# Attention on row halves: ScalarE's copy of a finished product placed behind the transposes' copies, fewer DMAs begun per step, and the weight decoding moved to another place in the loop

## The chip, the cores and the metric

The kernel runs on one core of a Trainium2 chip. The metric is the device time of one execution in microseconds; lower is better. The core's engines are named as the profile names them: PE (TensorE, the matrix engine; PEld are its weight loads), DVE (VectorE), ACT (ScalarE), POOL (GpSimd) and SP (SyncE, which here begins DMAs and passes semaphores on). Each engine runs its own instructions in the order in which they were written and meets the others through semaphores.

## What is computed

Attention with queries averaged in twos, then a dense feed-forward layer, then a layer that sends every token to one of eight experts:

```python
q_pool = q.reshape(B, H, S // 2, 2, D).mean(axis=3)      # B 4, H 8, S 1152, D 64
scores = q_pool @ k.T / sqrt(D)
attn = exp(scores - max) / (sum + 1e-9)
x = (attn @ v), laid out as 2304 tokens x 512
h = x @ w_in; g = piecewise(h); x = g @ w_out            # 512 -> 2048 -> 512
expert = argmax(normalised x @ normalised emb.T / tau)
out = gate * (relu(x @ w1[expert]) @ w2[expert])
```

## The kernel before

**Three stages.** The attention runs from the start to about 476 us, the dense layer behind it, the experts last. The change touches the attention loop (`Attention.run`) and what is done beside it.

**Pairs and steps.** The loop goes through 16 pairs of heads (n from 0 to 15). The 576 pooled queries of both heads of a pair make 1152 rows, which are nine tiles of 128 rows; each tile is one step (t from 0 to 8, s = 9n + t). Tile t = 4 holds 64 rows of either head, the **mixed tile**, and its scores take 18 matmuls where the others take 9. All matmuls work on 64 contracted rows, so that the upper and the lower half of the PE array each carry their own stream; where both halves write one PSUM bank, a `nop` on SP passes the semaphore from one half to the other (`relay`, `order`, L251 to L258; L254 in the profile is that `nop`). PE therefore can't go on with the second half before SP has come to the `nop`, and SP runs it in its own order, between the DMAs that it begins.

**What one step does.** PE writes the scores of tile t into the tile `sc` (three PSUM banks, one buffer). DVE reads them (`peak`, L265), writes them to SBUF as `e` and keeps the extreme of each row. ACT takes the exponential (`exp`, L272). PE transposes the `e` of two steps ago into `pa` and `pb` (`turn`, L289). ACT copies these, rounded, to `pth` (L307, two instructions), and DVE subtracts to get the rest, `ptl` (L309, two instructions). PE also works on `av`, the products of the transposed tiles with v: groups of 288 columns, four to a pair (`av_group`, L322), 36 matmuls each, fed into the steps from a queue. When the last matmul of a group is written, ACT's copy of it to `avs` (L329) is written at once, and after every second group four DMAs of `avs` are queued (`store`).

**Written order inside a step.** Scores with `av` matmuls between them; `peak`; the transposes with `av` matmuls between them; the copies and subtractions of `parts`; then `send`; further `av` matmuls; `exp`; and last `aside(s)`, which holds work of the later stages.

**SP's DMAs.** `later` puts a DMA into a list with the step from which it may go, and `send(3)` begins up to three of them at the place named above. In a steady pair these are eight stores of `avs` (`av_b`, `av_t`), four of the rows' sums (`rs`), four loads of q and one of v (`vr`).

**Decoding of weights.** `w_in` and `w_out` come as 64-bit numbers and are turned into 32-bit ones by DVE, 512 columns at a time in three instructions (`Weights.decode`: L556, L560, L564), followed by two instructions on POOL. For the first three of sixteen weight blocks (`EARLY`), that is 18 such DVE pieces, this happens beside the attention: in steps 74, 92 and 110 `ws.load` begins two 512 KB loads on SP directly, and in every step with s % 3 = 1 from step 76 on one piece is written, at the step's end.

**POOL** prepares q and k of the next pair (L180, L57, L182, L193) and splits v (L57, L214 of the tile `vh`) in the steps t = 2 and t = 7.

Of the kernel before, what the change touches and what calls it, by code (L numbers as in the profile page):

```python
# [46 lines left out]
EARLY = 3  # L47

GQ = 288
# [25 lines left out]
class Attention:  # L75
# [4 lines left out]
    def __init__(self, tc, q, k, v, xs, cn):  # L80
        self.tc, self.nc = tc, tc.nc
        self.q, self.k, self.v, self.xs, self.cn = q, k, v, xs, cn
        self.st = {}
        self.avq = [collections.deque() for _ in range(2)]
        self.queue = []

    def later(self, step, f):
        self.queue.append((step, f))
# [223 lines left out]
    def av_group(self, n, g):  # L312
        nc = self.nc
        h = g // 2
        c0 = g * GQ
        box = {}

        def mm(half, i):
            if half == i == 0:
                box["t"] = self.ps_v.tile([128, 512], F32, name="av", tag="av")  # L320
            p, r = (UP, LO)[half], self.pth if i < 9 else self.ptl
            m = nc.tensor.matmul(box["t"][:, 0:GQ], lhsT=self.vh[p, h * 9 + i % 9], rhs=r[p, i % 9, c0:c0 + GQ],  # L322
                                 start=half == i == 0, stop=half == 1 and i == 17)
            if half and i == 0:
                self.order(m, box["m"])
            if i == 17 and not half:
                box["m"] = self.relay(m)
            if i == 17 and half:
                nc.scalar.copy(self.avs[:, g * GQ:(g + 1) * GQ], box["t"][:, 0:GQ])  # L329
                if g % 2:  # L330
                    self.store(n, h)
            elif i == 17:
                self.avq[1].extend(lambda j=j: mm(1, j) for j in range(18))

        self.avq[0].extend(lambda j=j: mm(0, j) for j in range(18))

# [27 lines left out]
    def run(self, aside, tail, early):  # L364


        np_ = self.NPAIR
# [5 lines left out]
        g = collections.deque()  # L373
# [3 lines left out]
        for n in range(np_):  # L377
            for i in range(4):
                last = -(-GQ * (i + 1) // 128) - 1
# [5 lines left out]
        while s < nt + 1 or self.avq[0] or self.avq[1]:  # L385
            s += 1
            self.step = s
            n, t = divmod(s, 9)
            more = n + 1 < np_
            up = lo = ()  # L390
            if s < nt:
                if s > 3:
                    next(clear, None)
                if t in (2, 7):
                    self.split_v(n, t // 7)
                if more:
                    if t == 0:
                        sq.extend(self.split_qk(n + 1))
                    for _ in range(((2, 2, 0, 3, 1, 2, 1, 0, 3) if n else (0, 0, 0, 0, 3, 3, 2, 2, 4))[t]):
                        if sq:  # L400
                            sq.popleft()()
                    if t == 7:
                        self.later(s + 1, lambda n=n: self.load_v(n + 1))
                    for h, m in (((0, 1),) if s == 2 else ((1, 1),) if s == 3 else ()) + (
                            ((t // 7, n + 2),) if n + 2 < np_ and t in (3, 7) else ()):
                        if s == 3 and m == 1:
                            self.load_k(1, 1)
                        for p in (UP, LO):
                            self.later(s + (m > 1 and n == 0) * 4, lambda a=(m, h, p): self.load_q(*a))
                if s < 3:  # L410
                    self.warm(WARM[s])
                up, lo = self.scores(n, t)
            for a in ready.get(s, []):
                self.av_group(*a)
            count = 18 if s > nt + 1 else 6 if t in (2, 3, 4) else 9
            left = [count + held - 1, count]

            def av(half, m=1):
                for _ in range(min(m, left[half], len(self.avq[half]))):
                    left[half] -= 1  # L420
                    self.avq[half].popleft()()

            for f in lo[:1]:
                f()
            av(0, held)
            for i, f in enumerate(up):
                if i + 1 < len(lo):
                    lo[i + 1]()
                else:
                    av(1)  # L430
                f()
            if s < nt:
                self.peak(n, t)
            if 2 <= s < nt + 2:
                (a, b), ps = self.turn(*divmod(s - 2, 9))
                if s >= nt:
                    av(1, 4)
                for i in range(6):
                    b[i]()
                    a[i]()  # L440
                av(1)
                for i in (6, 7, 8):
                    a[i]()
                for _ in range(4):
                    av(1)
                    av(0)
                for i in (6, 7, 8):
                    b[i]()
                self.parts(*divmod(s - 2, 9), ps)
            go = s >= nt - 7 and len(g) > 0 and g[0][0]()  # L450
            self.send(3)
            while any(min(left[half], len(self.avq[half])) for half in range(2)):
                av(1)
                av(0)
            held = int(bool(self.avq[0]))
            if s < nt:
                self.exp(n, t)
            for f in first[s + 1] if s < 3 else ():
                f()
            if 9 <= s < nt + 9 and t == 0:  # L460
                self.divisor(n - 1)
            if 9 <= s < nt + 9 and t == 1:
                self.sums(n - 1)
            if s == nt - 1:
                self.ps_s.release()
                early()
            if s == nt - 9:
                self.prep.release()
                g.extend(tail())
            if go:  # L470
                for f in g.popleft()[1]:
                    f()
            aside(s)
# [1049 lines left out]
def tile_kernel(tc, q, k, v, w_in, w_out, emb, tau, w1, w2, out):  # L1523
    nc = tc.nc
    with ExitStack() as ctx:
# [19 lines left out]
        with ExitStack() as actx:  # L1545
# [8 lines left out]
            for h in range(2):  # L1554
                at.load_first(h)
            rt = Router(tc, one, dram, emb, tau, cn)
            last = (at.NPAIR - 1) * 9
            pieces = []

            def aside(s):  # L1560
                if s == 12:
                    late["consts"] = rt.consts(stage)
                if 12 <= s < 12 + 3 * 6 and s % 3 == 0:
                    next(late["consts"], None)
                if s == 28:
                    late["emb"] = rt.experts(stage)
                if s in (31, 34):
                    late["emb"][(s - 31) // 3]()
                j, c = divmod(s - (last - 63), 18)
                if 0 <= j < EARLY:  # L1570
                    if c == 2:
                        ws.load(j)
                    elif c == 3:
                        pieces.extend(ws.decode(j))
                if pieces and s % 3 == 1:
                    pieces.pop(0)()

            def tail():
                late["x0"] = tc.alloc_tile_pool(name="x0", bufs=1, side="right", reuse_waits="tile")
# [96 lines left out]
```

## Time and profile before

| | us |
|---|---|
| median of three runs | 1151.37 |
| lowest and highest | 1150.55, 1151.93 |
| the profiled execution's own time | 1153.7 |
| its span, first to last instruction | 1151.9 |

The profile is of one execution. Its span is cut into views: groups of instructions by line, waits (who waited for whom), and a timeline of single instructions with their start, their duration and, in square brackets, the idle time of the engine just before, and what ended it. PE's granted clock is given as a share of its full 2.4 GHz.

| engine | busy in the span |
|---|---|
| PE | 95% |
| DVE | 74% |
| ACT | 66% |
| POOL | 38% |

### The profile page before, as it was taken

The page shows a single profiled execution, that of the slowest core. Times are in us where ns is not written, and L with a number is a line of the kernel's source. Part 1 is how long each engine was busy: PE and PEld are TensorE (multiplying, and loading weights), DVE is VectorE, ACT ScalarE, POOL GpSimd, SP SyncE. Part 2 cuts the span into 40 slices and gives each one's busy share as a digit, 9 for nine tenths or more (in the row PEclk, how much of TensorE's full clock was granted, in tenths as well). Part 3 has the DMA queues.
Part 4 walks back from the last instruction along what each step waited for, and adds up shares of the span by engine and source line. Part 5 has one row for each costly group of instructions (what it writes and reads, how often), then busy time and mean ns, then how long its engine had stood idle before and what let it go on. Part 6 is the DMA issues. An engine that isn't in the chain of part 4 may idle for free.

```text
span 1151.9 us, 27178 instructions
## 1 busy us (share of the span) xinstructions
PE 1098.8 (95%) x10276; PEld 999.3 (87%) x10276; DVE 856.8 (74%) x1620; ACT 758.0 (66%) x1432; POOL 441.1 (38%) x473
## 2 busy tenths in 40 slices
PE   8999899999898899999999999999999999999997
PEld 6888888888888888899999989998989899988887
DVE  5989889889899998689856764665355666777775
ACT  4888888878787888655554445544446466667664
POOL 5987667767676774500002131112010231122211
PEclk8999999999999999999999999999999999999999
DMA  6454444454545436555521212120222121187444
GB/s 157 116 137 117 112 111 113 115 143 111 148 112 148 112 77 174 153 179 172 165 83 46 77 53 74 42 69 20 86 90 92 47 84 49 49 277 244 143 153 133
DMA packets 76855, 132.01 MB, mean 115 GB/s; under 512 B 21031, under 2 KB 39079, under 8 KB 76704
## 3 DMA queue, kind: packets, MB, share of 16 engines
q1 hardware_dynamic: 67856, 103.48, 31.6%
q0 software_dynamic: 8544, 26.31, 8.0%
q8 instruction: 88, 1.44, 0.5%
q14 instruction: 63, 0.52, 0.2%
q10 hardware_dynamic: 304, 0.26, 0.1%
HBM read 140.08 MB, written 20.08 MB: 139 GB/s over the span
## 4 chain that ended last, share of the span: by engine, by line
PE 74%; DVE 11%; issue 5%; ACT 4%; SPq 2%; DMA 2%; POOL 1%; POOLq 0%; DVEq 0%; ACTq 0%
PE h L687 18%; PE y L719 17%; PE sc L238 9%; PE av L322 8%; PE d_po L1396 7%; PE d_ph L1362 6%; DVE e L265 5%; DVE ptl L309 3%; PE pa L289 3%; SPq L361 1%; PE d_ph L1376 1%; ACT pth L307 1%; ACT e L272 1%; PE pb L289 1%; DMA out<-d_ob,d_rec 1%
## 5 line engine op out<-in xcount | busy, mean ns | idle before, releaser
L238 PE MATMUL sc<-kT,qt 64*128 64x384 f32 x1440 | 200.2, 352 | 30.2 <-DVE e L265 23.1
L265 DVE TENSOR_SCALAR_CACHE_REDUCE e<-sc 128x1152 f32<-128x1152 f32 x144 | 194.9, 1353 | 40.1 <-PE sc L238 37.8
L238 PEld LDWEIGHTS sc<-kT,qt 64*128 64x128 f32 x1440 | 150.3, 188 | 52.6 <-DVE e L265 31.4
L272 ACT ACTIVATE e<-e,nm 128x1152 f32<-128x1152 f32 x144 | 182.4, 1266 | 15.6 <-DVE e L265 15.1
L322 PE MATMUL av<-pth,vh 64*128 64x288 f32 x1152 | 150.1, 313 | 2.8 <-SPq L254 2.6
L309 DVE TENSOR_TENSOR ptl<-pa,pth 128x768 fp32r<-128x768 f32 x144 | 137.3, 954 | 17.8 <-ACT pth L307 16.4
L1302 DVE TENSOR_TENSOR e<-e,e 128x512 fp32r<-128x512 f32 x200 | 129.6, 688 | 26.6 <-ACT e L1301 16.1
L322 PE MATMUL av<-ptl,vh 64*128 64x288 f32 x1152 | 145.3, 311 | 0.0
L706 DVE SCALAR_TENSOR_TENSOR u<-h,u 128x320 f32<-128x320 f32 (+1 forms) x112 | 55.9, 499 | 115.0 <-ACT u L705 115.0
L702 ACT ACTIVATE u<-h,half 128x320 f32<-128x320 f32 (+1 forms) x112 | 59.8, 534 | 118.1 <-PE h L687 118.1
L307 ACT CAST pth<-pa 128x768 fp32r<-128x768 f32 x144 | 115.3, 801 | 31.1 <-PE pa L289 28.6
L322 PEld LDWEIGHTS av<-pth,vh 64*128 64x128 f32 x1152 | 119.6, 187 | 6.8 <-SPq L254 6.7
L1396 PE MATMUL d_po<-e,e 128*128 128x512 f32 x504 | 120.6, 393 | 0.0
L322 PEld LDWEIGHTS av<-ptl,vh 64*128 64x128 f32 x1152 | 118.0, 187 | 0.0
L1301 ACT CAST e<-e 128x512 fp32r<-128x512 f32 x200 | 113.8, 620 | 0.3 <-issue 0.3
L719 PE MATMUL y<-wh,gh 128*128 128x512 f32 x288 | 113.9, 395 | 0.0
L719 PE MATMUL y<-wh,gl 128*128 128x512 f32 x288 | 113.7, 395 | 0.0
L719 PE MATMUL y<-wl,gh 128*128 128x512 f32 x288 | 113.6, 394 | 0.0
L1396 PEld LDWEIGHTS d_po<-e,e 128*128 128x128 f32 x504 | 92.8, 188 | 18.1
L289 PE MATMUL pb<-idf,e 64*128 64x64 f32 x864 | 101.2, 224 | 0.3
L652 POOL TENSOR_TENSOR xl<-xth,xl 128x512 f32<-128x512 f32 (+1 forms) x9 | 11.2, 1244 | 225.8 <-DMA xl<-av_b 127.6
L289 PE MATMUL pa<-idf,e 64*128 64x64 f32 x1728 | 88.7, 224 | 9.3 <-DVE ptl L309 9.2
(253 smaller groups left out, 2357.8 us busy)
## 6 DMA issues: line engine op xcount, KB each, us to landing
e<-moe_w SPq DMA_DIRECT2D x104, 512.0 KB
qr<-q SPq DMA_DIRECT2D x62, 288.0 KB
kr<-k POOLq DMA_DIRECT2D x60, 192.0 KB, 3.4
vr<-v SPq DMA_DIRECT2D x16, 576.0 KB
av_b<-avs SPq DMA_DIRECT2D x64, 128.0 KB
raw<-moe_w_in SPq DMA_DIRECT2D x14, 512.0 KB
raw<-moe_w_out SPq DMA_DIRECT2D x14, 512.0 KB
yt<-emb_rows SPq DMA_DIRECT2D x24, 256.0 KB
```

Source lines behind the costliest of these rows:

```text
L238: i = nc.tensor.matmul(s[:, j, 0:384], lhsT=qt[p, w, c:c + 128], rhs=d["kT", h][p, r], start=start, stop=stop)
L265: self.nc.vector.tensor_scalar(out=e.rearrange("p (a b) -> p a b", a=3), in0=d["sc"][:, :, 0:384], scalar1=-0.5 / D ** 0.5, scalar2=None, ...
L272: self.nc.scalar.activation(e, e, AF.Exp, bias=d["nm"][:, t:t + 1], scale=-1.0, accum_out=d["sum"][:, t:t + 1])
L289: x = nc.tensor.transpose(o, e[p, i * 128:(i + 1) * 128], idf[p, p])
L307: nc.scalar.copy(hi, p)
L309: nc.vector.tensor_sub(out=lo, in0=p, in1=hi.bitcast(F32))
L322: m = nc.tensor.matmul(box["t"][:, 0:GQ], lhsT=self.vh[p, h * 9 + i % 9], rhs=r[p, i % 9, c0:c0 + GQ], start=half == i == 0, stop=half == ...
L687: nc.tensor.matmul(ps[:, :n], lhsT=a[:, k], rhs=b[:, k, h0:h0 + n], start=i == 0, stop=i == 11)
L719: self.nc.tensor.matmul(y, lhsT=a, rhs=b, start=j == 0 and q == 0, stop=j == NF - 1 and q == 2)
L1301: self.nc.scalar.copy(hi, r)
L1302: self.nc.vector.tensor_sub(out=lo, in0=r, in1=hi.bitcast(F32))
L1396: self.nc.tensor.matmul(self.o, lhsT=(self.hh, self.hl)[a][f // 4][:, f % 4, s], rhs=self.w[b, f // 2][:, f % 2], start=f == 0 and q == 0, ...
```

## The change

Three edits, all in the attention.

**The copy.** Where the last matmul of a group is written, the copy to `avs` is no longer written at once but put into the list `full`, which the loop empties after `send` and the `av` matmuls behind it, ahead of `exp`. Three of a pair's four groups end behind `parts` already, so their copies stay where they were. The third group of the pair before ends early in step t = 4, ahead of `parts`; its copy moves behind the two copies to `pth`.

**The sends.** `send(3)` becomes `send(2)`, except in steps t = 3 and in the last pair, where it stays at three. The 17 DMAs of a pair have 19 places, where they had 27.

**The decoding.** The loads go through `later`, one part of 512 KB at a time, from step 37 on, each next one after the piece that frees its buffer. The pieces are written at the end of each step t = 3, that is ahead of the mixed tile's `peak`, from step 39 on, and from step 78 on also at the end of each step t = 6. Of the 18 pieces 11 stand at t = 3 and 7 at t = 6; the last is in step 132 (before: 127).

```diff
-                nc.scalar.copy(self.avs[:, g * GQ:(g + 1) * GQ], box["t"][:, 0:GQ])
-                if g % 2:
-                    self.store(n, h)
+                self.full.append(lambda: out(box["t"]))
...
+        def out(t):
+            nc.scalar.copy(self.avs[:, g * GQ:(g + 1) * GQ], t[:, 0:GQ])
+            if g % 2:
+                self.store(n, h)
...
-            self.send(3)
+            self.send(3 if t == 3 or n + 1 >= np_ else 2)
             while any(min(left[half], len(self.avq[half])) for half in range(2)):
                 av(1)
                 av(0)
             held = int(bool(self.avq[0]))
+            while self.full:
+                self.full.pop(0)()
...
+            def decode():
+                def load(part):
+                    at.later(at.step + 1, lambda: ws.load(*divmod(part, 2)))
+
+                def pieces():
+                    for j in range(EARLY):
+                        for i, f in enumerate(ws.decode(j)):
+                            f()
+                            part = 2 * j + i // 3 + 2
+                            if i % 3 == 2 and part < 2 * EARLY:
+                                load(part)
+                            yield
+                for part in range(2):
+                    load(part)
+                return pieces()
...
-                j, c = divmod(s - (last - 63), 18)
-                if 0 <= j < EARLY:
-                    if c == 2:
-                        ws.load(j)
-                    elif c == 3:
-                        pieces.extend(ws.decode(j))
-                if pieces and s % 3 == 1:
-                    pieces.pop(0)()
+                if s == 36:
+                    late["decode"] = decode()
+                if s > 36 and (s % 9 == 3 or s > 72 and s % 9 == 6):
+                    next(late["decode"], None)
```

ACT in steps t = 3 and t = 4 of pair 2, before; the first `exp` is that of the tile t = 3.

```order
L272 ACTIVATE e,sum<-e,nm 128x1152 [waits DVE_49,Activation_49]
L329 COPY avs<-av 128x288 [waits DMAHW4_49,DMAHW3_49,DMAHW5_49,DMAHW2_49,PE_49]
L307 CAST pth<-pa 128x2x6x64
L307 CAST pth<-pb 128x2x3x64 [waits PE_49]
L272 ACTIVATE e,sum<-e,nm 128x1152 [waits DVE_49,Activation_49]
```

The same place of the change:

```order
L272 ACTIVATE e,sum<-e,nm 128x1152 [waits DVE_49,Activation_49]
L307 CAST pth<-pa 128x2x6x64 [waits PE_49]
L307 CAST pth<-pb 128x2x3x64 [waits PE_49]
L334 COPY avs<-av 128x288 [waits DMAHW4_49,DMAHW5_49,DMAHW3_49,DMAHW2_49]
L272 ACTIVATE e,sum<-e,nm 128x1152 [waits DVE_49,Activation_49]
```

The copy and the two copies to `pth` have changed places; the `exp` of tile t = 4 now follows the copy.

DVE in pair 9 from the `peak` of tile t = 3 to that of t = 5, before; `wf` is a decoding piece.

```order
L265 TENSOR_SCALAR e,nm<-sc 128x1152
L309 TENSOR_TENSOR ptl<-pa,pth 128x2x6x64
L309 TENSOR_TENSOR ptl<-pb,pth 128x2x3x64
L265 TENSOR_SCALAR e,nm<-sc 128x1152
L309 TENSOR_TENSOR ptl<-pa,pth 128x2x6x64
L309 TENSOR_TENSOR ptl<-pb,pth 128x2x3x64
L556 TENSOR_SCALAR wf<-raw 128x512
L265 TENSOR_SCALAR e,nm<-sc 128x1152
```

The same place of the change:

```order
L265 TENSOR_SCALAR e,nm<-sc 128x1152
L309 TENSOR_TENSOR ptl<-pa,pth 128x2x6x64
L309 TENSOR_TENSOR ptl<-pb,pth 128x2x3x64
L561 TENSOR_SCALAR wf<-raw 128x512
L265 TENSOR_SCALAR e,nm<-sc 128x1152
L309 TENSOR_TENSOR ptl<-pa,pth 128x2x6x64
L309 TENSOR_TENSOR ptl<-pb,pth 128x2x3x64
L265 TENSOR_SCALAR e,nm<-sc 128x1152
```

The piece stands one tile earlier, between the subtractions of step t = 3 and the mixed tile's `peak`. PE's instructions keep their order in the whole program.

SP around the first pair of raw loads, before (steps t = 8 of pair 7 to t = 5 of pair 8; the `nop`s aren't shown):

```order
L165 DMA vr<-v 128x2x576
L153 DMA qr_4636<-q 64x1152 x2
L361 DMA av_b_73<-avs 64x512
L361 DMA av_t_76<-avs 64x64
L361 DMA av_b_73<-avs 64x512
L507 DMA raw<-moe_w_in 128x4x256
L512 DMA raw<-moe_w_out 128x1024
L361 DMA av_t_76<-avs 64x64
L351 DMA rs_b_79<-rt 9x32 x4
```

The same place of the change, and what is there now:

```order
L165 DMA vr<-v 128x2x576
L153 DMA qr_4718<-q 64x1152 x2
L364 DMA av_b_73<-avs 64x512
L364 DMA av_t_76<-avs 64x64
L364 DMA av_b_73<-avs 64x512
L364 DMA av_t_76<-avs 64x64
L354 DMA rs_b_79<-rt 9x32 x4
```

The two raw loads are gone from between the stores, which are begun in steps t = 2 and t = 3; `vr` is begun in step t = 0 of pair 8 (before: t = 8 of pair 7), with a q load behind it.

## Rows read from the trace of the kernel before

**Rows 1.** The page's head, and its busy times of the engines.

```profile
span 1151.9 us, 27178 instructions
PE 1098.8 (95%) x10276; PEld 999.3 (87%) x10276; DVE 856.8 (74%) x1620; ACT 758.0 (66%) x1432; POOL 441.1 (38%) x473
```

**Rows 2.** All peaks (duration min/median/max, first and last start); then busy times of stretches.

```profile
L265 DVE TENSOR_SCALAR_CACHE_REDUCE e<-sc x144: 1315/1358/1360, 10.0 to 465.2; 128x1152 f32<-128x1152 f32 x144
...
67.10:94.20 27.10, 25.69 (x402) 24.12 (x399) 24.59 (x38) 23.86 (x42) 22.27 (x36) 1.00 0.51 135
322.80:351.30 28.50, 25.68 (x404) 24.11 (x401) 26.54 (x41) 24.18 (x42) 21.07 (x23) 1.00 0.45 112
...
500.00:520.00 20.00, 20.00 (x113) 18.02 (x112) 17.28 (x35) 10.46 (x23) 0.00 (x0) 1.00 0.57 180
```

**Rows 3.** Timeline of DVE in pair 2: start, duration, instruction, idle time before.

```profile
67.09 1.36 DVE L265 TENSOR_SCALAR_CACHE_REDUCE e<-sc 128x1152 f32<-128x1152 f32 x1 [0.40 <-PE sc L238]
...
69.83 1.36 DVE L265 TENSOR_SCALAR_CACHE_REDUCE e<-sc 128x1152 f32<-128x1152 f32 x1
...
75.75 1.36 DVE L265 TENSOR_SCALAR_CACHE_REDUCE e<-sc 128x1152 f32<-128x1152 f32 x1 [0.28 <-PE sc L238]
...
79.21 1.36 DVE L265 TENSOR_SCALAR_CACHE_REDUCE e<-sc 128x1152 f32<-128x1152 f32 x1 [0.76 <-PE sc L238]
...
81.39 0.96 DVE L309 TENSOR_TENSOR ptl<-pa,pth 128x768 fp32r<-128x768 f32 x1 [0.81 <-ACT pth L307]
...
82.73 1.35 DVE L265 TENSOR_SCALAR_CACHE_REDUCE e<-sc 128x1152 f32<-128x1152 f32 x1
...
85.42 1.36 DVE L265 TENSOR_SCALAR_CACHE_REDUCE e<-sc 128x1152 f32<-128x1152 f32 x1
...
94.23 1.36 DVE L265 TENSOR_SCALAR_CACHE_REDUCE e<-sc 128x1152 f32<-128x1152 f32 x1 [0.37 <-PE sc L238]
```

**Rows 4.** Timeline of ACT in steps t = 4 and t = 5 of pair 2.

```profile
80.25 0.40 ACT L329 COPY avs<-av 128x288 f32<-128x288 f32 x1 [1.60 <-PE av L322]
80.55 0.81 ACT L307 CAST pth<-pa 128x768 fp32r<-128x768 f32 x1
81.25 0.49 ACT L307 CAST pth<-pb 128x384 fp32r<-128x384 f32 x1
81.61 1.28 ACT L272 ACTIVATE e<-e,nm 128x1152 f32<-128x1152 f32 x1
...
83.03 0.80 ACT L307 CAST pth<-pa 128x768 fp32r<-128x768 f32 x1
```

**Rows 5.** Waits in the attention: engine, line, waited for; total, times, longest.

```profile
POOL vh L57 <- PE av L322: 58.6, 15, 8.0
...
PEld sc L238 <- SPq L254: 14.0, 29, 1.5
...
POOL vh L57 <- DMA vr<-v: 9.0, 4, 2.6
```

**Rows 6.** Timeline of SP in pair 2: a third DMA of t = 2, and `vr`.

```profile
74.39 0.59 SPq L361 DMA_DIRECT2D av_b<-avs  x1
...
92.34 0.53 SPq L165 DMA_DIRECT2D vr<-v  x1
```

**Rows 7.** Timeline at the first raw loads (pair 8), and a stretch behind them.

```profile
242.70 0.48 SPq L512 DMA_DIRECT2D raw<-moe_w_out  x1
243.29 0.18 PEld L238 LDWEIGHTS sc<-kT,qt 64*128 64x128 f32 x1 [1.31 <-SPq L254]
...
245.00:249.00 4.00, 4.00 (x50) 4.00 (x49) 2.38 (x5) 2.00 (x4) 3.77 (x4) 0.71 0.91 293
```

**Rows 8.** The decoding pieces of DVE in the attention: duration min/median/max, first and last start.

```profile
L556 DVE TENSOR_SCALAR wf<-raw x6: 417/882/1529, 251.9 to 397.9; 128x512 uint32<-128x512 uint32 x6
L560 DVE SCALAR_TENSOR_TENSOR wf<-raw,wf x6: 1003/1009/1023, 260.4 to 407.5; 128x512 uint32<-128x512 uint32 x6
L564 DVE SCALAR_TENSOR_TENSOR wf<-raw,wf x6: 649/649/651, 270.1 to 417.3; 128x512 uint32<-128x512 uint32 x6
```

**Rows 9.** Timeline of POOL and of DVE at a piece in pair 10.

```profile
309.26 1.42 POOL L182 TENSOR_TENSOR qt<-qr,qt 128x576 fp32r<-128x576 f32 x1
```

```profile
309.87 1.09 DVE L556 TENSOR_SCALAR wf<-raw 128x512 uint32<-128x512 uint32 x1
```

More of the change, by code (lines that the diff above doesn't have):

```diff
@@ L84, in __init__ @@
         self.avq = [collections.deque() for _ in range(2)]
-        self.queue = []
+        self.queue, self.full = [], []
     def later(self, step, f):
@@ L1556, in tile_kernel @@
             rt = Router(tc, one, dram, emb, tau, cn)
-            last = (at.NPAIR - 1) * 9
-            pieces = []
+            def decode():
[12 more added lines that the diff above has]
+                return pieces()
             def aside(s):
```

## The prediction

> **What bounds the kernel now.** First the table of stretches [rows 2]: from 500 us on PE is busy 20.00 of 20 us, so from there on an earlier start is an earlier end by as much, and nothing in the change touches that part. The question is therefore how long the attention takes, and the last of its 144 peaks begins at 465.2 us [rows 2], of a span of 1151.9 [rows 1]. In the attention no engine is full: in pair 2, which no piece of decoding disturbs, PE is busy 25.69, DVE 24.59 and ACT 23.86 of 27.10 us [rows 2], and PE's busy time counts matmuls that overlap. What runs is a ring: DVE's peak frees `sc`, PE writes the next scores, DVE takes the next peak. The time between two starts of L265 is the step. Where DVE does nothing but its peak and two subtractions a step takes 69.83 - 67.09 = 2.74 or 85.42 - 82.73 = 2.69 us [rows 3]: DVE is the bound there. The rest is idle time of DVE, and the timeline names its end: 0.40 and 0.37 ahead of the peaks of t = 0, 0.28 ahead of t = 3, 0.76 ahead of t = 4, each for PE's scores, and 0.81 in t = 4 for ACT [rows 3]. The 0.76 is the mixed tile's double work on PE and stays. The other three are what the first two edits are about.
>
> **The copy.** In step t = 4 ACT stands idle 1.60 us ahead of the copy, until PE has done the last `av` matmul, and only then does the copy (0.40) and the two copies to `pth` (0.81 and 0.49) [rows 4]. `pa` is long there: in the next step the copy to `pth` begins 83.03 - 82.73 = 0.30 behind the peak [rows 3, 4], here 80.55 - 79.21 = 1.34. DVE waits 0.81 for it, and the step takes 82.73 - 79.21 = 3.52 instead of 2.7 [rows 3]. After the change `pth` comes at 0.30 behind the peak, about a microsecond earlier, and DVE's wait of 0.81 goes. What is late next? ACT's own turn: from 79.51 it does 0.81, 0.49, the copy 0.40 and an `exp` of 1.28, 2.98 together, and comes to the next `pa` at 82.49. The next peak would be at 79.21 + 2.71 = 81.92, and would want it at 82.22. ACT is 0.27 late, which at worst DVE waits for. So 0.54 to 0.81 a pair, and I take 0.70, since ACT's instructions overlap a little at their ends (81.61 is ahead of 81.25 + 0.49) [rows 4]. Fifteen pairs have such a copy (1 to 15): 15 x 0.70 = **10.5 us**, with 8.1 and 12.2 as the near ends. Should ACT stay late through the later copies of the pair, 0.3 is left of it, 4.5 us; ACT's 23.86 of 27.10 [rows 2] leave room, so I don't expect that. Who waits for the copy itself? It frees one of two `av` buffers, and the group that wants it begins two steps later; its DMAs come only after the next group.
>
> **The sends.** SP's `nop` stands behind the DMAs of the step. In t = 2 the third of them runs from 74.39 to 74.98 [rows 6], and behind it PE's second half is late; the peak of t = 3 finds DVE idle for 0.28, and that of t = 0, behind `vr` and loads of q, for 0.37 to 0.40 [rows 3]. All such waits of PE's weight loads for SP are 14.0 us in 29 places [rows 5]. With two DMAs the third's 0.6 us leaves the way of the `nop`, which is more than either wait. So 0.28 + 0.37 = 0.65 a pair for the pairs without decoding from 2 to 8: 7 x 0.65 = **4.5 us**. In pairs 9 to 13 DVE is late by its pieces and these waits are hidden; there I count nothing. The high end is all 14 pairs, 9 us; the low end 0, if a pair of DMAs still covers the `nop` in t = 0, where `vr` and a q load now go together, or in t = 3 with its three.
>
> **The raw loads.** In steps 74, 92 and 110 two loads go on SP behind the three of `send`, five in a row. At the first PE waits 1.31 us, and in the four microseconds behind it the granted clock is 0.71, so some of that stretch was at 1.2 GHz instead of 2.4 [rows 7]. Each of the three now goes within the two of a step. Saved: 1.31 less the usual 0.28 at the first, about half of that at the other two, and up to (1 - 0.71) x 4.0 = 1.2 of the clock: about **3.5 us**, from 1.5 (the waits of the first alone and little else) to 4.3 (three times 1.03 and all of the clock).
>
> **The decoding.** A pair with three pieces takes 28.50 against 27.10 [rows 2], 0.47 a piece of mean 0.85 [rows 8], because the pieces also fill DVE's waits. Eighteen pieces are 8.4, and about 1 more for first pieces that were longer than the least (L556: 0.42 to 1.53) [rows 8]: 9.4 us now. After the change 11 stand ahead of the mixed tile's peak, where DVE is idle for 0.76 in any case [rows 3]. Three are L564 with 0.65 and free, four L556 with a median of 0.88 (0.12 over), four L560 with 1.01 (0.25 over): 1.5 us. Seven stand at t = 6, ahead of a peak that has no idle time [rows 3], three L564, two L560, two L556: 5.7 us at full price, 3.4 at the share that a piece costs now. Together 5 to 7; saved **4 us**, from 2 to 4.5. POOL's two instructions behind every third piece stay as many.
>
> A piece can be held up, though. At 309.87 an L556 that takes 0.42 at best took 1.09; POOL's instruction beside it ran from 309.26 to 310.68 [rows 8, 9], and the piece ended 0.28 behind that. The Trainium skill (SBUF — State Buffer, section SBUF: two separate sides) states that a DVE instruction in a two-port mode, or with two SBUF inputs, and a GpSimd instruction lock one port pair against each other for their whole length, so that the later one waits; the trace agrees in this place. That would speak against the mixed tile, where POOL works without a pause; what it would give here is the second rival.
>
> **Sum.** 10.5 + 4.5 + 3.5 + 4 = 22.5 us. The profiled execution would go from 1153.7 to about 1131, the median, 2.3 lower, from 1151.4 to **1129**. All best ends give 30 (1121), all worst (4.5, 0, 1.5 and 0 for the decoding) 6 (1145).
>
> **Rivals.**
> *ACT takes DVE's place.* With the waits gone, ACT's four copies of a pair make its steps longer than 2.7, and the wait moves from t = 4 to t = 5 and on. Against it: 3.2 us of idle ACT in 27.1 [rows 2]. The copy then gives 4.5, the sum 16.5: 1135. Chance 0.17.
> *The pieces meet POOL.* If each of the 11 at the mixed tile takes as long as the longest L556, 1.53, then 0.77 of each is over, 8.5 instead of 1.5: the sum is 15.5, 1136. For it: POOL is busy 22.27 of 27.10 [rows 2], and rows 9. Against it: the least L556 of 0.42, and L564 always at 0.65 [rows 8]. Chance 0.13.
> *The sends do nothing.* The `nop` still comes too late, since a step's two DMAs take 1.1 us and the places are now 19 for 17. Then the first and last terms alone, and half of the raw loads': 1135 to 1140, say 1137. Chance 0.11.
> *`vr` comes too late, on the other side.* It was begun at 92.34 [rows 6], ahead of t = 0; it now goes a step later, 2.7 us. POOL waited for it already in 4 places, 9.0 us [rows 5]. Splitting v, and behind it q and k of the next pair, would begin up to 2.7 later in each pair. POOL has 27.1 - 22.3 = 4.8 us of room a pair [rows 2], and waits 58.6 us in 15 places for PE at the same instruction [rows 5]. The mechanism decides from the point where POOL's extra wait is more than those 4.8 in a pair; at 2 us over it in 14 pairs it costs 28 and the kernel takes 1157. Chance 0.04.
> *The change does next to nothing:* each idle time only moves to the next wait of the ring. Within 1149 to 1153. Chance 0.03.
> The forecast has the remaining 0.52.
>
> **How the numbers follow.** The range takes in the forecast with its best ends, with 2 us beyond for waits that shorten with the ring, and the first three rivals with room for two of them at once: 1119 to 1143. Beyond 0.2% (2.3 us, about what a measurement of this kernel can tell from no change) faster are the forecast and the first three rivals, 0.93; the same 0.03; slower 0.04.
>
> **What would show it.** In the profile after: the wait of L309 for ACT's L307 in t = 4 gone, and the step t = 4 to t = 5 at 2.7 to 2.9 instead of 3.5; if it is right but the next step has grown by 0.3 or more, the first rival. No idle time of DVE of 0.28 and 0.37 ahead of t = 3 and t = 0, and PE's waits for SP well under 14 us; if not, the third. No half clock after 240 us. L561 (the old L556) over 1.1 in several pieces of t = 3, with the mixed step over 3.5: the second. POOL's wait for `vr` far over 9 us, with the peaks of t = 0 or t = 4 waiting for q or k: the fourth. The forecast is wrong if the last peak begins later than 453, or if it begins near 443 and the end doesn't follow it, for then something behind the attention isn't bound by PE.

## The result and the profile after

| us | before | after |
|---|---|---|
| median (runs) | 1150.96 (4) | 1120.99 (4) |
| lowest and highest | 1149.44, 1151.93 | 1117.32, 1124.47 |
| span of the profiled execution | 1151.9 | 1119.8 |
| the last peak begins | 465.2 | 433.5 |
| behind that | 686.7 | 686.3 |

The changed kernel takes 0.974 of the time of the one before (95% interval 0.9707 to 0.9774), 30 us less, where 22.5 were forecast. The last two rows of the table show where: the attention is 31.7 us shorter, and what stands behind it is as long as it was.

The page's head and busy times, after, answer to [rows 1]:

```profile
span 1119.8 us, 27167 instructions
PE 1088.0 (97%) x10276; PEld 998.8 (89%) x10276; DVE 852.2 (76%) x1620; ACT 754.9 (67%) x1432; POOL 441.6 (39%) x473
```

The peaks (duration min/median/max, first and last start) and then busy times of stretches (length, PE, PEld, DVE, ACT, POOL, granted clock, DMA share, GB/s), after, answer to [rows 2]:

```profile
L265 DVE TENSOR_SCALAR_CACHE_REDUCE e<-sc x144: 1311/1357/1359, 9.8 to 433.5; 128x1152 f32<-128x1152 f32 x144
...
64.90:90.50 25.60, 24.79 (x400) 24.05 (x398) 24.50 (x39) 23.61 (x42) 22.40 (x37) 1.00 0.52 141
...
100.00:430.00 330.00, 315.44 (x4912) 300.18 (x4909) 314.03 (x491) 296.69 (x512) 246.45 (x255) 1.00 0.50 133
```

Pair 2 takes 25.60 us instead of 27.10 with nearly the same busy times of DVE and ACT (24.50 and 23.61; before 24.59 and 23.86): what went is idle time. DVE is now busy for 96% of the pair. The clock is at its upper level, 2.4 GHz, all through the stretch from 100 to 430 us, and the stretch with 0.71 of [rows 7] has no counterpart.

DVE in pair 2, after (start, duration, instruction, idle time before), against [rows 3]:

```profile
65.14 1.36 DVE L265 TENSOR_SCALAR_CACHE_REDUCE e<-sc 128x1152 f32<-128x1152 f32 x1
...
73.56 1.36 DVE L265 TENSOR_SCALAR_CACHE_REDUCE e<-sc 128x1152 f32<-128x1152 f32 x1
...
77.05 1.36 DVE L265 TENSOR_SCALAR_CACHE_REDUCE e<-sc 128x1152 f32<-128x1152 f32 x1 [0.78 <-PE sc L238]
...
78.33 0.95 DVE L309 TENSOR_TENSOR ptl<-pa,pth 128x768 fp32r<-128x768 f32 x1
...
79.68 1.36 DVE L265 TENSOR_SCALAR_CACHE_REDUCE e<-sc 128x1152 f32<-128x1152 f32 x1
...
90.75 1.36 DVE L265 TENSOR_SCALAR_CACHE_REDUCE e<-sc 128x1152 f32<-128x1152 f32 x1
```

The 0.81 ahead of L309 in t = 4 is gone, so the step from 77.05 to 79.68 takes 2.63 instead of 3.52. The idle time of 0.28 ahead of the peak of t = 3 is gone too, and those of 0.40 and 0.37 ahead of the two peaks of t = 0 are down to 0.13. Of the 1.10 us in which DVE is still idle in this pair (25.60 - 24.50) 0.78 stand ahead of the mixed tile's peak, PE's double work.

ACT in the same place, after, against [rows 4]:

```profile
77.39 0.80 ACT L307 CAST pth<-pa 128x768 fp32r<-128x768 f32 x1 [0.94 <-PE pa L289]
78.28 0.48 ACT L307 CAST pth<-pb 128x384 fp32r<-128x384 f32 x1
78.65 0.41 ACT L334 COPY avs<-av 128x288 f32<-128x288 f32 x1
78.94 1.27 ACT L272 ACTIVATE e<-e,nm 128x1152 f32<-128x1152 f32 x1
...
80.19 0.80 ACT L307 CAST pth<-pa 128x768 fp32r<-128x768 f32 x1
```

`pth` is begun 77.39 - 77.05 = 0.34 behind the peak (before 1.34). The next `pth` begins 80.19 - 79.68 = 0.51 behind its peak, where [rows 3, 4] had 0.30: ACT is 0.2 late, and DVE hardly feels it, as its own L309 can't begin before its peak of 1.36 ends.

Waits up to 450 us (total, times, longest), after, against [rows 5]:

```profile
POOL wh L57 <- DVE wf L569: 19.0, 6, 6.3
POOL vh L57 <- PE av L322: 17.9, 9, 4.3
POOL vh L57 <- DMA vr<-v: 14.0, 8, 3.1
...
PEld sc L238 <- SPq L254: 7.3, 14, 1.4
...
DVE ptl L309 <- ACT pth L307: 3.4, 3, 1.8
```

PE's waits for SP in this row are halved (14.0 in 29 before). The later load of v shows as 14.0 us of waiting in place of 9.0, but POOL waits 17.9 us for PE at the same instruction, so there still is room.

The decoding pieces, after, against [rows 8]:

```profile
L561 DVE TENSOR_SCALAR wf<-raw x6: 415/420/639, 128.8 to 375.0; 128x512 uint32<-128x512 uint32 x6
L565 DVE SCALAR_TENSOR_TENSOR wf<-raw,wf x6: 681/828/1464, 155.8 to 392.7; 128x512 uint32<-128x512 uint32 x6
L569 DVE SCALAR_TENSOR_TENSOR wf<-raw,wf x6: 680/680/681, 181.9 to 401.6; 128x512 uint32<-128x512 uint32 x6
```

The first two instructions have become shorter (medians 882 to 420 and 1009 to 828 ns), the third takes 680 ns instead of 649. Taking the least duration of each as its length (0.42 and 0.68 us), the twelve instructions of the first two rows were 5.2 us longer than that before and are 1.6 us longer now. What held them is shown by the experiments with three more DVE instructions.

### The profile page after: what moved, and what is told of

The parts are those of the page before. It is cut to its first block, busy times and chain, and to the rows that moved or that the text cites. A ratio compares the mean times of both kernels' runs of the same rounds, so it can differ in the third digit from the quotient of the medians.

```text
span 1119.8 us, 27167 instructions
## 1 busy us (share of the span) xinstructions
PE 1088.0 (97%) x10276; PEld 998.8 (89%) x10276; DVE 852.2 (76%) x1620; ACT 754.9 (67%) x1432; POOL 441.6 (39%) x473
## 3 DMA queue, kind: packets, MB, share of 16 engines
q8 instruction: 88, 1.44, 0.6%
## 4 chain that ended last, share of the span: by engine, by line
PE 73%; DVE 14%; issue 5%; POOL 2%; SPq 2%; DMA 2%; ACT 2%; POOLq 0%; DVEq 0%; ACTq 0%
PE h L692 18%; PE y L724 18%; PE sc L238 9%; DVE e L265 9%; PE d_po L1401 8%; PE d_ph L1367 7%; PE av L322 6%; DVE ptl L309 3%; PE pa L289 2%; PE d_ph L1381 1%; SPq L364 1%; DMA out<-d_ob,d_rec 1%; PE pb L289 1%; PE d_pt L1346 1%; POOL kT L193 1%
## 5 line engine op out<-in xcount | busy, mean ns | idle before, releaser
L265 DVE TENSOR_SCALAR_CACHE_REDUCE e<-sc 128x1152 f32<-128x1152 f32 x144 | 194.6, 1352 | 26.2 <-PE sc L238 23.1
L238 PE MATMUL sc<-kT,qt 64*128 64x384 f32 x1440 | 191.6, 350 | 18.5 <-DVE e L265 14.1
L322 PE MATMUL av<-pth,vh 64*128 64x288 f32 x1152 | 145.2, 311 | 2.3 <-SPq L254 2.2
L309 DVE TENSOR_TENSOR ptl<-pa,pth 128x768 fp32r<-128x768 f32 x144 | 137.3, 953 | 4.3 <-ACT pth L307 3.4
L713 ACT CAST gh<-u 128x320 fp32r<-128x320 f32 (+1 forms) x112 | 52.4, 468 | 66.2 <-DVE u L711 66.1
```

The source lines that it names most:

```text
L238: i = nc.tensor.matmul(s[:, j, 0:384], lhsT=qt[p, w, c:c + 128], rhs=d["kT", h][p, r], start=start, stop=stop)
L265: self.nc.vector.tensor_scalar(out=e.rearrange("p (a b) -> p a b", a=3), in0=d["sc"][:, :, 0:384], scalar1=-0.5 / D ** 0.5, scalar2=None, ...
L309: nc.vector.tensor_sub(out=lo, in0=p, in1=hi.bitcast(F32))
```

## The experiments

Two theories were tested. **Separate waits:** each edit takes away an idle time of DVE at its own place, so each is worth its own amount alone and the amounts add. **Interlocked waits:** the idle times belong to one ring, so one edit alone moves a wait on, and only all three together pay.

Single executions of one kernel differ by some microseconds (1133.8 to 1139.0 in the first run below), so amounts are taken from the ratios, which go by several executions (1% is 11.5 us), and places from the profiles.

### One edit alone

Each part of the change is put into the kernel before by itself. The copy:

```diff
-                nc.scalar.copy(self.avs[:, g * GQ:(g + 1) * GQ], box["t"][:, 0:GQ])
...
+                self.full.append(lambda: out(box["t"]))
...
+            while self.full:
+                self.full.pop(0)()
```

> The kernel before with the first edit alone: the copy to avs behind the two copies to pth. Theory of separate waits (each edit takes away an idle time of DVE at a place of its own, and the gains add): the step from the mixed tile's peak to the next goes from 3.52 to about 2.65 us in all 15 pairs that have such a copy, 0.85 x 15 = 12 to 13 us, a ratio near 0.989; the waits for SP ahead of t = 0 and t = 3 stay at 0.3 to 0.4. Rival, interlocked waits (a wait taken away alone comes back at the next one of the ring, so that only all three edits together bring the gain): the step is shorter but the next ones grow, less than 6 us in all, a ratio above 0.995.

The sends:

```diff
-            self.send(3)
+            self.send(3 if t == 3 or n + 1 >= np_ else 2)
```

> The kernel before with the second edit alone: two DMAs a step. Separate waits: DVE's idle times ahead of t = 0 and t = 3 go in pairs 2 to 8, 0.65 to 0.7 each, about 5 us, in pairs 9 to 13 little, since DVE is late there by its pieces; and the raw loads stand behind two DMAs instead of three, 0.6 us in three places: 6 to 7 us, a ratio near 0.994. Interlocked: nothing, 0.998 or more.

The decoding, with the change's `decode`:

```diff
...
-                if pieces and s % 3 == 1:
-                    pieces.pop(0)()
...
+                if s > 36 and (s % 9 == 3 or s > 72 and s % 9 == 6):
+                    next(late["decode"], None)
```

> The kernel before with the third edit alone: raw loads through the list, pieces ahead of the mixed tile and at t = 6. Separate waits: the pieces cost 3 to 4 us instead of 9, the raw loads' waits of 3.5 go, but in pairs 9 to 13 the waits for SP, hidden by the pieces until now, come to light (5 x 0.65): 9 - 3 = 6 us, a ratio near 0.995. Interlocked: half of that or less.

Measured: copy 0.9892 (0.9860 to 0.9924, 12.4 us), sends 0.9912 (0.9877 to 0.9947, 10.1 us), decoding 0.9911 (0.9880 to 0.9942, 10.2 us). The copy came as expected; the sends and the decoding gave more than the 6 to 7 and the 6 us expected of them. Together the three are 32.7 us, where the whole change gives 29.9. Each of these amounts is known to some 4 us either way, and within that they add: the interlocked theory, which wanted nothing or half from one edit alone, falls. Where each acts is seen in the steps, the time from the peak before to the peak of t, medians of pairs 2 to 7 and, on the right, of pairs 9 to 13 (from the starts of L265):

| us | t=0 | t=3 | t=5 | t=8 | 9-13: t=0 | t=2 | t=5 | t=7 | t=8 |
|---|---|---|---|---|---|---|---|---|---|
| before | 3.08 | 2.94 | 3.52 | 3.01 | 2.82 | 3.56 | 4.53 | 2.72 | 3.74 |
| copy alone | 3.09 | 2.95 | 2.64 | 3.01 | 2.81 | 3.56 | 3.31 | 2.73 | 3.74 |
| sends alone | 2.82 | 2.69 | 3.52 | 2.81 | 2.82 | 3.56 | 3.99 | 2.73 | 3.74 |
| decoding alone | 3.09 | 2.95 | 3.52 | 3.01 | 3.07 | 2.99 | 3.52 | 3.21 | 2.64 |
| all three | 2.83 | 2.69 | 2.63 | 2.80 | 2.82 | 2.99 | 2.63 | 3.22 | 2.62 |

The copy changes t = 5 and nothing else in pairs 2 to 7; PE's waits for SP stay at 14.1 us in 28 places with it. The sends change t = 0, 3 and 8, and from pair 8 on mainly the steps with raw loads (t = 3 of pairs 8, 10 and 12, 4.15 to 3.47, 3.79 to 3.11, 3.59 to 2.90) and t = 5. The decoding changes only the right half, where three of the steps become shorter by 0.57 to 1.10 us: the pairs 8 to 11 take 27.2 to 27.5 us with their pieces (27.6 and 28.7 in pairs 12 and 13), hardly more than pair 2 without a piece (27.2).

The gain of the sends at t = 5 of pairs 9 to 13 (4.53 to 3.99) is of another kind. The decoding piece there is an L556, and with the sends alone the six of them are shorter than before (882 and 1529 ns in [rows 8]):

```profile
L556 DVE TENSOR_SCALAR wf<-raw x6: 417/496/652, 243.5 to 387.2; 128x512 uint32<-128x512 uint32 x6
```

Before, three of them began 0.18 to 0.62 us behind POOL's L182 and ended 0.28 behind its end; with the sends alone none begins while an L182 runs. That is 2.6 us of this profile, a gift of the altered timing and not of the edit's mechanism. The copy alone and the raw loads alone (below) got 1.8 and 2.0 us in the same way. Such a gain can be had only once, so the single amounts hold a part in common; one trace of each kernel doesn't tell how large it is in other executions.

In DVE's timeline of the kernel with the decoding alone (pair 12) a piece at the mixed tile stands ahead of a peak that waits for PE in any case:

```profile
348.05 1.36 DVE L265 TENSOR_SCALAR_CACHE_REDUCE e<-sc 128x1152 f32<-128x1152 f32 x1 [0.29 <-PE sc L238]
...
350.67 0.42 DVE L556 TENSOR_SCALAR wf<-raw 128x512 uint32<-128x512 uint32 x1
351.50 1.36 DVE L265 TENSOR_SCALAR_CACHE_REDUCE e<-sc 128x1152 f32<-128x1152 f32 x1 [0.42 <-PE sc L238]
```

351.50 - 348.05 = 3.45, as long as the mixed step without a piece: the piece came out of the wait, 0.42 of which is left. In this kernel the waits for SP come back in pairs 9 to 13 (t = 0 from 2.82 to 3.07): the pieces had hidden them.

### All but one edit

Here each part is taken out of the changed kernel, and the other two stay. The copy is written at once again:

```diff
-                self.full.append(lambda: out(box["t"]))
+                nc.scalar.copy(self.avs[:, g * GQ:(g + 1) * GQ], box["t"][:, 0:GQ])
...
```

> The change without its first edit. Separate waits: 0.85 x 15 = 12 to 13 us slower than the change, near 1133.5, a ratio to the kernel before near 0.985. Interlocked: the copy's wait holds the ring back in every pair, so that most of the 30 us is lost: over 1142.

Three sends in every step:

```diff
-            self.send(3 if t == 3 or n + 1 >= np_ else 2)
+            self.send(3)
```

> The change with send(3) in every step. Separate waits: the idle times ahead of t = 0, t = 3 and t = 8 come back in 14 pairs, 0.65 each, 9 us: near 1130, a ratio to the kernel before near 0.982. Interlocked: over 1140.

Pieces and raw loads at their old places:

```diff
-                if s > 36 and (s % 9 == 3 or s > 72 and s % 9 == 6):
-                    next(late["decode"], None)
...
+                if pieces and s % 3 == 1:
+                    pieces.pop(0)()
```

> The change with the old decoding: raw loads on SP directly, four DMAs in a row with the two of a step, pieces at every third step. Separate waits: 18 pieces at about 0.45 each, 8 us instead of 2 to 3, and three waits of about 0.7: 7 to 8 us slower than the change, near 1128.5, a ratio near 0.980. Interlocked: over 1140.

Measured: without the copy 0.9825 (0.9791 to 0.9859), without the sends 0.9826 (0.9800 to 0.9853), without the decoding 0.9811 (0.9791 to 0.9831). Against 0.974 that is 9.8, 9.9 and 8.2 us for each, 27.9 together; separate waits had 12 to 13, 9, and 7 to 8, interlocked ones 19 or more. Without the copy, t = 5 is at 3.51 again; without the sends, t = 0, 3 and 8 are at 3.08, 2.94 and 3.01, in pairs 9 to 13 too (3.07 and 2.95 at t = 0 and 3). Without the decoding it is the right half's t = 2, 5 and 8 that are long again (3.56, 3.21 and 3.75). Each wait comes back at its own places, and no other median of these kernels is more than 0.11 above the change's.

### The raw loads alone

In the kernel before, only the raw loads go through the list, one at a time, by the change's `decode`; the pieces stay and `send(3)` stays.

```diff
...
+                if s == 66:
+                    late["decode"] = decode()
+                if s > 75 and s % 3 == 1:
+                    next(late["decode"], None)
```

> The kernel before with the raw loads alone changed: through the list, part by part, from step 66 on; the pieces stay at every third step, send(3) stays. Splits the third edit. If the raw loads' place on SP and the half clock behind the first are worth 3.5 us, as the prediction has it: a ratio near 0.997, and no half clock after 240 us. If the pieces' place is all that counts: 1.000 within 0.001.

Measured 0.9973 (0.9960 to 0.9986): 3.1 us. From 240 to 250 us the granted clock is 1.00. Before, it was 0.58 from 244 to 248 us. So of the 10.2 us of the third edit about 3 are the loads and about 7 the place of the pieces, each known to a few microseconds only.

### Two DMAs in t = 3 as well

```diff
-            self.send(3 if t == 3 or n + 1 >= np_ else 2)
+            self.send(3 if n + 1 >= np_ else 2)
```

> The change with two DMAs in the steps t = 3 too (18 places for 17 and a half). In the change the mixed tile's step is 3.45 to 3.5 us in undisturbed pairs but 3.7 to 4.05 in some where an av_t among the three DMAs of t = 3 took 1.1 to 1.5 us to begin. If the number of DMAs is what exposes such a slow one, these steps fall to 3.5 and the kernel is 1 to 3 us faster than the change. If the two that are left cover the slow one as badly, or the list is too full now and v or q come later, the same within 2 us or slower by up to 3.

Measured 1117.66 us, 0.9715 (0.9690 to 0.9740); the last peak begins at 429.4. The interval overlaps that of the change, so it is a gain of about 3 us or none. The mixed step is at 3.47 and 3.48 in both groups of pairs (3.48 and 3.68 in the change), which is where the third DMA stood.

### The load of v two steps later

```diff
-                        self.later(s + 1, lambda n=n: self.load_v(n + 1))
+                        self.later(s + 3, lambda n=n: self.load_v(n + 1))
```

> The change with the load of v two steps later still, in step t = 1. Tests the rival in which a late v reaches PE through POOL. Room theory: POOL waits some 4 us longer for v in each pair, 60 us in all instead of 14, takes it out of its waits for PE, and the time stays within 0.3% of the change. Rival: q and k of the next pair come late, PE waits for POOL, and the kernel is slower by 1 us or more a pair, over 1135.

Measured 1126.31 us, 0.9795 (0.9777 to 0.9814), 5 to 6 us slower than the change. The waits up to 450 us:

```profile
POOL vh L57 <- DMA vr<-v: 36.6, 9, 7.9
...
POOL vh L57 <- PE sc L238: 18.3, 5, 5.1
```

POOL waits for `vr` 22.6 us more than in the change, yet the steps of pairs 2 to 13 are the same but for some tenths at t = 4 (3.65 and 3.89). Neither expectation met it: the room is used up in the last pair alone, in which and behind which 5.6 of the profile's 6.6 us stand. There PE waits 1.62 us for POOL's split of v (L214) up to 441.27, the granted clock is 0.69 in the stretch from 440 to 444, and pair 15 takes 30.40 us instead of 28.67. The fourth rival's mechanism is real, and it begins to cost about two steps beyond where the change put the load.

### Three more DVE instructions in a step

39 short additions of two SBUF tiles (128x64, their result unused), three in each of pairs 2 to 14, at the end of step t = 3 in one kernel (shown) and of t = 6 in the other (`s % 9 == 6`):

```diff
+                if 18 <= s < 135 and s % 9 == 3:
+                    for _ in range(3):
+                        nc.vector.tensor_add(out=spare, in0=zero, in1=zero)
```

> The change with three more DVE instructions of about 0.2 us (0.5 to 0.6 together, their result unused) at the end of each step t = 3 of pairs 2 to 14, 13 times. Measures the price of DVE work ahead of the mixed tile. If DVE's idle time of about 0.75 there hides it: within 1.5 us of the change, and only in the pairs that also have a decoding piece there (11 of 13) does the step grow, by 0.4 at most where the two together pass 0.75: up to 4 us. If it isn't hidden: 13 x 0.55 = 7 us slower.

> The same three DVE instructions at the end of each step t = 6 instead. There DVE has no idle time, so the next step should grow by the full 0.5 to 0.6, and the one behind it should shrink by up to 0.2 (as 2.80 goes to 2.62 behind the decoding pieces): 13 x 0.35 to 0.55 = 5 to 7 us slower than the change. If a pair has slack behind the step in any case: under 2 us.

Measured at t = 3: 1137.91 us, 0.9892 (0.9871 to 0.9913), 17 us slower than the change. At t = 6: 1156.51 us, 1.0052 (1.0032 to 1.0071), 35 us slower, and slower than the kernel before. Both miss their expectations by far, since 39 instructions of 0.22 us are only 8.6 us. They weren't all of 0.22 us: together they took 17.1 us at t = 3 and 25.8 at t = 6. The groups of the two kernels, t = 3 first (duration min/median/max in ns):

```profile
L1591 DVE TENSOR_TENSOR spare<-zero x39: 214/225/1470, 75.8 to 405.4; 128x64 f32<-128x64 f32 x39
```

```profile
L1591 DVE TENSOR_TENSOR spare<-zero x39: 214/575/1479, 82.9 to 431.7; 128x64 f32<-128x64 f32 x39
```

DVE and then POOL of the second kernel, pair 2, step t = 6:

```profile
82.89 2.54 DVE L1591 TENSOR_TENSOR spare<-zero 128x64 f32<-128x64 f32 x3
85.36 1.34 DVE L265 TENSOR_SCALAR_CACHE_REDUCE e<-sc 128x1152 f32<-128x1152 f32 x1
```

```profile
82.94 1.46 POOL L214 TENSOR_TENSOR vh<-vr,vh 128x576 fp32r<-128x576 f32 x1
84.36 1.94 POOL L193 TENSOR_TENSOR kT<-kr,kT 128x384 fp32r<-128x384 f32 x2
```

Three instructions take 2.54 us instead of 0.66. Singly they are 0.22 (begun at 82.89, ahead of POOL's L214), 1.33 (ended at 84.48, 0.08 behind the end of L214 at 84.40) and 0.92 (ended at 85.43, 0.07 behind the first L193). Over both kernels, the 32 that no POOL instruction touches in time (the DMAs that POOL begins left out) take 0.21 to 0.23 us, and the 46 beside one take up to 1.48: a DVE instruction that reads two SBUF tiles and begins second waits until POOL's ends. The peaks (L265) and the subtractions (L309), which read PSUM, don't show it: the longest of the 144 subtractions of `pa` takes 0.96 us in this kernel, the least 0.94. The Trainium skill (SBUF — State Buffer, section SBUF: two separate sides) states this lock: whichever begins first has the port pair for its whole instruction. The trace agrees, and gives the price here: up to 1.26 us for an instruction of 0.22.

At t = 6 POOL's split of v (L214) begins within 0.12 us of the first of the three in 8 of 13 pairs, and 29 of 39 had a POOL instruction beside them. At t = 3 it was 17, and there three pairs (5, 11 and 14) grew by 3.7 to 4.8 us each, which is most of the loss.

A second cost follows the first. In the profile with t = 6 the last peak is 30.5 us later than in the change; 27.1 of them stand in the steps t = 7, about the length of the added instructions, and 5.8 in the steps t = 0, which come two steps later and have no added instruction (the rest of the attention is 2.4 us shorter). In pair 2 (stretches as above, then DVE):

```profile
84.00:88.00 4.00, 2.02 (x32) 1.78 (x30) 3.96 (x7) 2.01 (x4) 3.69 (x6) 1.00 0.29 80
88.00:92.00 4.00, 4.00 (x45) 3.98 (x43) 2.79 (x5) 2.30 (x6) 3.83 (x7) 0.57 0.51 134
```

```profile
92.32 1.36 DVE L265 TENSOR_SCALAR_CACHE_REDUCE e<-sc 128x1152 f32<-128x1152 f32 x1 [1.18 <-PE sc L238]
```

While DVE is held, PE is busy for 2.02 of 4 us; in the next 4 us its granted clock is 0.57, and the peak of t = 0 waits 1.18 us for it. From 60 to 440 us the clock is 0.97 in this kernel, where the change has 1.00.

### The rows' sums on POOL's queue

The longest pair of the change is the last (28.67 us). To two DMAs in every step this adds that the eight loads of the rows' sums in that pair are begun by POOL:

```diff
...
-                    load(r[64 * h:64 * h + 64, ks, a1:e1], rs.to_broadcast([64, ks.stop - ks.start, e1 - a1]))
+                    load(r[64 * h:64 * h + 64, ks, a1:e1], rs.to_broadcast([64, ks.stop - ks.start, e1 - a1]),
+                         self.nc.sync if g else self.nc.gpsimd)
```

> The change with two DMAs in every step of a pair (as in e8_two_always), and in the last pair the eight loads of the rows' sums (L615) begin on POOL's DMA queue and not on SyncE's. The last pair is the one place where the steps stayed long: 28.67 us in the change and 29.03 in e8_two_always, where a clean pair takes 25.6; its long steps (3.84 ahead of t=6, 3.35 ahead of t=7, 3.63 ahead of t=2) stand behind steps in which SyncE begins three DMAs. If SyncE's queue is the cause there, eight DMAs of some 0.6 us leave it, and the last pair falls by 1 to 2.5 us: 1115 to 1116.5 us where e8_two_always measured 1117.7, with the last pair between 26.5 and 28. Rival: POOL's own work (its splits of v and the products' last pieces) stands ahead of these loads, so they begin late and the tiles of the projection behind the attention wait for them: 1118 to 1121, with the last pair at 29 or the span behind the last peak longer than 686.5.

Measured 1119.16 us, 0.9715 (0.9693 to 0.9738): no better than two DMAs always. Both theories were half right. The last pair fell to 26.41 us and its last peak begins at 428.0, so its DMAs on SP's queue were what made it long. But PE then meets POOL (PE's timeline; POOL's; stretches as above):

```profile
433.83 1.32 PE L322 MATMUL av<-pth,vh 64*128 64x288 f32 x7 [1.96 <-POOL vh L214]
```

```profile
431.60 0.68 POOL L57 TENSOR_SCALAR vh<-vr 128x576 fp32r<-128x576 f32 x1
```

```profile
428.00:432.00 4.00, 3.27 (x55) 2.81 (x50) 2.78 (x5) 4.00 (x10) 3.92 (x4) 1.00 0.17 39
432.00:436.00 4.00, 2.17 (x18) 2.17 (x20) 1.17 (x2) 1.32 (x3) 3.84 (x4) 0.69 0.16 37
```

The eight DMAs that POOL begins take it 0.62 us each. Four of them stand in a stretch, from 418 us on, in which POOL works without a pause up to the last split of v; that begins at 431.60, 1.9 us later than with two DMAs always (429.71). PE waits 1.96 us for it, and its clock is 0.69 in that stretch. Behind the last peak stand 689.4 us instead of 686.5; the gain is given back there.

## Why the prediction was right, and where its terms were off

The time lies in the range and on the right side, and the signs it named appeared: L309's wait gone, the step at 2.63, no idle time of 0.28 and 0.37, waits for SP halved, no lower clock after 240 us. The last peak begins 31.7 us earlier and the end follows it by 32.1, so the first part, that an earlier start of the dense stage is an earlier end, holds to half a microsecond. The size was forecast too small: 30 us were measured, 22.5 forecast. 30 is what the prediction gave for all of its best ends together, 2 us inside the low end of its range. The sends make up most of the difference.

**The copy** (10.5 forecast; 12.4 alone, 9.8 as the last of three). Right mechanism. A clean pair gains 3.52 - 2.63 = 0.89, not 0.70: I took off for ACT being late, and ACT is late by 0.2 without DVE waiting for it. 15 x 0.89 = 13.4 lies near the single run. The first rival (1135) is out: t = 6 goes from 2.70 to 2.73 only.

**The sends** (4.5; 10.1 alone, 9.9 as the last). This is the term that was mis-sized most, by two steps of its working. I priced t = 0 and t = 3 and left out t = 8, which gains 0.21 a pair. And "in pairs 9 to 13 ... I count nothing" holds for the kernel before, where the pieces hide those waits (t = 0 at 2.82), but not for the changed kernel, in which the third edit takes the pieces away from there: without the sends, these pairs show 3.07 and 2.95. On the changed kernel it is 0.25 at t = 0 and at t = 3 in 14 pairs and 0.21 at t = 8 in seven, 8.5 us, next to the high end of 9 that I gave. The third rival (1137) is out.

**The raw loads** (3.5). 3.1 measured (1.6 to 4.6), with the shorter L556 of that run in it.

**The decoding** (4; about 7, from 10.2 less 3.1; as the last of three 8.2 with the loads, so about 5). The gain came in part for a reason that the sum doesn't have. I read L560's 1.01 as the length of the instruction, and held that 0.25 of it would be over at the mixed tile and all of it at t = 6. It is 0.68 long, and was held up at its old place: all six in the kernel before stand beside POOL's L193, the one at 260.42 ends 0.55 behind it (DVE, then the two L193 of POOL, before):

```profile
260.42 1.01 DVE L560 SCALAR_TENSOR_TENSOR wf<-raw,wf 128x512 uint32<-128x512 uint32 x1
```

```profile
258.91 1.97 POOL L193 TENSOR_TENSOR kT<-kr,kT 128x384 fp32r<-128x384 f32 x2
```

At its new places it has a median of 828 and four of six are at most 835. A piece at t = 6 costs 0.49 in its own step (3.22 against 2.73) and gives 0.18 back in the next (2.62 against 2.80), so 0.3 and not 0.8. Pieces that POOL holds up less are up to 3.6 us of the gain (5.2 less 1.6); the prediction counted about 1 us of that, for L556. A slip of its sum is small: seven pieces at 0.47 are 3.3, not 3.4.

**The pieces meet POOL** (second rival, 1136). Not what happened, yet real. One L565 took 1.46 us (DVE, then POOL, after):

```profile
155.81 1.46 DVE L565 SCALAR_TENSOR_TENSOR wf<-raw,wf 128x512 uint32<-128x512 uint32 x1
```

```profile
155.30 1.42 POOL L180 TENSOR_TENSOR qr<-qr 128x576 f32<-128x576 f32 x1
```

It ended 0.55 behind POOL's, as L560 did, and that step took 4.01 us. I looked only at how often pieces had been long, and gave 0.77 us for each as the worst. The added instructions show that what decides is which POOL instruction begins just ahead. In the change 8 of 18 pieces have no POOL instruction beside them at all (its DMAs left out), among them all six L569, behind which POOL waits (19.0 us in 6 places); four of the other ten began ahead of POOL's and kept their length.

**`vr` too late** (fourth rival). Not at one step later; at three steps it costs 5 to 6 us, nearly all of it in and behind the last pair, and not 28 in all pairs. The room of 4.8 us a pair was read rightly; that the last pair has less, since POOL there also does the products' rows, I had not looked at.

What of the waits for SP is left has a pattern that I did not foresee. DMAs of SP that take over 1.1 us to begin, with a median of 0.47, are 14 of 248 between 60 and 425 us. One of them (SP, then DVE, after, pair 10):

```profile
284.72 1.46 SPq L364 DMA_DIRECT2D av_t<-avs  x1
```

```profile
283.61 1.36 DVE L265 TENSOR_SCALAR_CACHE_REDUCE e<-sc 128x1152 f32<-128x1152 f32 x1
...
287.66 1.36 DVE L265 TENSOR_SCALAR_CACHE_REDUCE e<-sc 128x1152 f32<-128x1152 f32 x1 [0.76 <-PE sc L238]
```

The step takes 4.05 us where its like take 3.48. Why these DMAs are slow to begin was not tried and stays open.

## What to carry to other kernels

Cost each part of a change on the kernel that has the other parts: a wait that a neighbour hides today is free to remove only until the neighbour moves. Where one engine is the bound, put extra work just ahead of the place where it waits in any case, and look up what the other engine of a shared port does at that moment. On a queue that passes semaphores on, count the DMAs ahead of the semaphore, not the bytes: here a load of 512 KB took SP 0.48 us to begin [rows 7], a 64 x 64 store 1.46.

## What the runs showed of the hardware

- A DVE instruction with two SBUF inputs took 0.21 to 0.23 us by itself in 32 cases and up to 1.48 us behind a POOL instruction, ending 0.07 to 0.09 us behind it. A decoding piece with one SBUF input (L556, 0.42 at least) was held as well, up to 1.53 us [rows 8]. POOL is held the other way round: L214, 1.41 to 1.44 us in 28 of 32 places of the change, took 1.68 to 1.95 in the four where a piece had begun just ahead of it.
- One DMA costs its beginner 0.47 us on SP (median) and 0.62 us on POOL (the eight loads of the rows' sums), so moving DMAs from SP to a busy POOL moves the wait along with them.
- Where PE waited 1.6 and 2.0 us in the last pair (the load of v two steps later, the sums on POOL's queue), the granted clock of the 4 us around the wait's end was 0.69, so part of it was at 1.2 GHz. Behind DVE's hold-up with three more instructions at t = 6 it was 0.57 in pair 2, and PE's next scores came 1.18 us late.
